# Sixteen-byte offsets for the operands of an MLP's matmuls

## The chip, the cores and the metric

One core of a Trainium2 chip runs the whole program. The metric is the device time of one execution in microseconds, the median of several runs.

## The reference

Retention attention feeds two MLPs. The second one, which the change touches, is in fp32:

```python
def _moe2_ref(x, w_in, w_out):          # x: 2304 x 512, w_in: 512 x 2048, w_out: 2048 x 512
    h = x @ w_in
    neg, pos = h <= -1.0, h >= 1.0
    g = np.where(pos, h, np.where(neg, 0.0, (h + 1.0) ** 2 / 4.0))
    return (g @ w_out).astype(np.float32)
```

## The kernel before

All work is issued in an order written out by hand, the list ORDER: a word such as `hp.7.2` calls the step `hp_` with arguments 7 and 2. Engines take their instructions in that order, and semaphores between tiles do the rest. Attention and the first MLP fill the first 276 us or so; the second MLP runs from there to the end, at first together with the last of the first MLP.

Every fp32 product of the second MLP is made of three TensorE matmuls, since each operand is split in a high and a low part of type fp32r (high times low, low times high, high times high). The matrices are multiplied by a scheme with seven products instead of eight per 2x2 blocks: operands are stored as seven combinations, and the weights' combinations were computed earlier and put into DRAM (`wid` and `wod`, one piece for each of eight groups of 256 hidden units).

There are 32 main steps, four blocks of 512 tokens by eight groups. Step s does:

- `wi` and `wo` (both through `load_for` and `load14`) load 14,336 bytes a partition, the seven combinations of one group's weights, high and low, with one DMA on SP's queue. Three buffers hold weights of each kind. A new load takes the buffer of the step three before, so the weights rotate through homes named by pool and tag: w0 and w1 of pool w1i and wo2 of pool wos for the weights in, wo0 and wo1 of pool wos and ln of pool act1 for the weights out. Near the end weights out come to the homes of weights in, too.
- `hp_` (its matmuls are L753) makes 42 matmuls: the weights are the stationary operand, 128x128, and a tile `xs` of tokens the moving one, 256 columns.
- `ha`, `hA`, `hB`, `hr_`, `hm`, `hq`, `hg`, `hf` on ScalarE and VectorE apply the activation and make the seven combinations of its result.
- `hh` on ScalarE and `hl` on VectorE split them into the gates' high and low part, two tiles that `ghl_tiles` gives out. They alternate with the step: tags w0 and w1 of pool w1o in even steps, w2 and w3 in odd ones.
- `pp` (L841, through `product`) makes 42 matmuls: now the gates are stationary, and the weights out the moving operand, 256 columns.

In the order list the matmuls of `pp` for an earlier step lie between those of `hp_`, a few at a time. The last 256 tokens have steps of their own: `tp` (L923) for the first product and `tj` (L841 again) for the second, with gates made by `ty` and `tz`.

Where a buffer lies modulo 256 bytes follows from the pads of 64 and 224 bytes at the foot of the two memory stacks, from tile sizes, which are multiples of 256 for nearly all tiles, and from the offset `o` in `load14`, counted in elements of four bytes. As built, all stationary tiles of the second MLP start at 0 modulo 256 (weights in, gates) and all moving ones at 192 (tokens, weights out). In each matmul the moving operand less the stationary one is then 192, and slices inside the tiles are multiples of 512 bytes.

Of the kernel before, what the change touches and what calls it, by code (L numbers as in the profile page):

```python
# [12 lines left out]
F32R = mybir.dt.float32r  # L13
# [10 lines left out]
DM = H * D  # L24
F1, F2 = 1024, 2048
P = 128
# [194 lines left out]
def net(ctx: ExitStack, tc: tile.TileContext, qk_t, kv, w_in1, w_out1, g_ln, w_in2, w_out2, masks, decay, out):  # L221
# [11 lines left out]
    w1i = ctx.enter_context(tc.tile_pool(name="w1i", bufs=1, side="right"))  # L233
    w1o = ctx.enter_context(tc.tile_pool(name="w1o", bufs=1, side="right"))
    const = ctx.enter_context(tc.tile_pool(name="const", bufs=1, side="right"))
    act1 = ctx.enter_context(tc.tile_pool(name="act1", bufs=1, side="right"))
# [173 lines left out]
    raw_w, wd, yd, rd, w_in1_sb, wo1, ws, w2x, w1s = {}, {}, {}, {}, [None] * KD, [None] * (C1 // 2), {}, {}, {}  # L410
# [255 lines left out]
    def load14(kind, p, home):  # L666
        pool, tag = home
        n, pools = 2 * 7 * 2 * P, {"w1i": w1i, "wos": wos, "act1": act1}
        x = pools[pool].tile([P, n + 64 * (pool != "act1")], F32R, tag=tag, name=kind)
        o = {"w1i": 0, "wos": 16, "act1": 0}[pool] if kind == "wi" else {"w1i": 48, "wos": 0, "act1": 0}[pool]  # L670
        x = x[:, o : o + n]
        x = x.rearrange("p (w i f) -> p w i f", w=2, f=2 * P)
        nc.sync.dma_start(x.bitcast(F32), (wid if kind == "wi" else wod)[p])
        resident[kind][p] = x, (pool, tag)

    def load_for(kind, s):
        full = len(resident[kind]) == 3
        if kind == "wo" and s == len(slots) - 1:
            home = resident["wi"].pop(slots[s - 2][1])[1]
        else:  # L680
            home = resident[kind].pop(slots[s - 3][1])[1] if full else homes[kind, s]
        load14(kind, slots[s][1], home)
# [9 lines left out]
    @step  # L692
    def wt(p):
        kind, old = {4: ("wi", 1), 5: ("wi", 0), 6: ("wo", TAIL[0]), 7: ("wo", TAIL[1])}[p]
        load14("wo", p, resident[kind].pop(old)[1])
# [112 lines left out]
        nc.vector.tensor_tensor(out=g[:, o], in0=g[:, x], in1=g[:, y], op=op)  # L808

    def ghl_tiles(i, n):  # L810
        return [w1o.tile([P, 7, n, P], F32R, tag=f"w{2 * (i % 2) + w}", name="g" + "hl"[w]) for w in range(2)]

    @step
    def hh(s, k):
        if k == 0:
            ghl[s] = ghl_tiles(s, 2)
        i = slice(4 * k, 4 + 3 * k)
        nc.scalar.activation(ghl[s][0][:, i], gs[s][:, i], AF.Copy)  # L818
# [189 lines left out]
    with tc.manual_schedule():  # L1008
        for word in ORDER.split():
            name, *args = re.split("[.]", word.rstrip("+"))  # L1010
            f = steps[name] if name in steps else steps[name + "_"]
# [43 lines left out]
```

## Time and profile before

| | us |
|---|---|
| median of 3 runs | 661.94 (661.71 to 668.92) |
| profiled execution | 662.21 |
| its span | 660.0 |
| granted TensorE clock, mean | 0.999 |
| TensorE busy | 651.8 |
| VectorE busy | 529.3 |
| ScalarE busy | 446.1 |

The span goes from the first to the last instruction of the profiled execution. TensorE's work is counted in matmuls (PE) and weight loads into the array (PEld), which run beside the matmuls. Matmuls overlap as well: one of 276 ns begins about 113 ns after the one before it, so a time from start to start says more than a duration.

### The profile page before, as it was taken

The numbers are of one execution on the slowest core, as the hardware profiler recorded it, in microseconds if no ns is written. First come the engines' busy times: TensorE is split into PE (matmuls) and PEld (weight loads), VectorE is DVE, ScalarE is ACT, GpSimd is POOL, SyncE is SP. The second block draws the span as 40 slices with busy tenths as digits, with TensorE's granted clock in tenths as the row PEclk, the third lists the DMA queues.
The fourth block names the chain that finished last, engine by engine and source line by source line (L and its number), as shares of the span: only waits on it lengthen the run. The fifth ranks groups of instructions, "written<-read, shape, count | busy, mean of one in ns | idle before, by whom it ended". The sixth has DMA issues, their size and how long they took to land.

```text
span 660.0 us, 14294 instructions
## 1 busy us (share of the span) xinstructions
PE 651.8 (99%) x5697; PEld 615.5 (93%) x5697; DVE 529.3 (80%) x1037; ACT 446.1 (68%) x806; POOL 180.4 (27%) x180
## 2 busy tenths in 40 slices
PE   9999999999999999999999999999999999999997
PEld 7888898998989898899999999999999999999997
DVE  4999898897997789936588879687888877766887
ACT  5678786768776776875667765676756766666642
POOL 5896765545565458510000000000000000000000
PEclk9999999999999999999999999999999999999999
DMA  8986386687986767999895756967497463677986
GB/s 321 392 301 256 131 293 263 230 274 273 409 295 222 249 266 265 387 337 404 324 411 200 308 221 214 345 236 279 184 355 281 182 223 118 250 302 292 366 305 236
DMA packets 34802, 184.85 MB, mean 280 GB/s; under 512 B 3760, under 2 KB 8496, under 8 KB 28208
## 3 DMA queue, kind: packets, MB, share of 16 engines
q1 hardware_dynamic: 34448, 183.65, 75.1%
q8 instruction: 45, 0.74, 0.4%
q10 hardware_dynamic: 288, 0.30, 0.2%
q14 instruction: 21, 0.17, 0.1%
HBM read 143.04 MB, written 40.89 MB: 279 GB/s over the span
## 4 chain that ended last, share of the span: by engine, by line
PE 80%; DVE 11%; DMA 5%; issue 1%; POOL 1%; ACT 1%; SPq 0%; DVEq 0%; POOLq 0%; ACTq 0%
PE bank L841 27%; PE bank L753 24%; PE bank L528 8%; PE bank L630 8%; PE bank L923 3%; PE bank L280 2%; DVE ws L455 2%; DVE ws L497 2%; PE bank L322 2%; PE bank L352 2%; DMA st<-in_w_in 2%; PE bank L340 2%; PE bank L600 1%; DVE sm L538 1%; DMA wod<-ws 1%; DMA kv<-in_kv 1%
## 5 line engine op out<-in xcount | busy, mean ns | idle before, releaser
L753 PE MATMUL bank<-xs,wi 128*128 128x256 f32 x1344 | 177.0, 280 | 0.7 <-ACT hc L770 0.7
L753 PEld LDWEIGHTS bank<-xs,wi 128*128 128x128 f32 x1344 | 164.3, 188 | 2.2 <-ACT hc L770 1.3
L841 PE MATMUL bank<-wo,gh 128*128 128x256 f32 x896 | 160.9, 278 | 0.0
L841 PEld LDWEIGHTS bank<-wo,gh 128*128 128x128 f32 x896 | 136.4, 189 | 0.0
L841 PE MATMUL bank<-wo,gl 128*128 128x256 f32 x448 | 124.8, 279 | 0.0
L528 PE MATMUL bank<-wi,x 128*128 128x512 f32 x432 | 104.7, 397 | 0.0
L630 PE MATMUL bank<-ln,wo 128*128 128x256 f32 x864 | 103.1, 279 | 0.6 <-DVE xf L379 0.6
L630 PEld LDWEIGHTS bank<-ln,wo 128*128 128x128 f32 x864 | 100.8, 188 | 1.8 <-DVE xf L379 0.8
L528 PEld LDWEIGHTS bank<-wi,x 128*128 128x128 f32 x432 | 79.4, 188 | 17.5 <-issue 0.8
L841 PEld LDWEIGHTS bank<-wo,gl 128*128 128x128 f32 x448 | 84.1, 188 | 0.2
L824 DVE TENSOR_TENSOR gl<-gs,gh 128x1024 fp32r<-128x1024 f32 (+1 forms) x64 | 69.3, 1088 | 15.5 <-ACT gh L818 15.3
L440 POOL TENSOR_TENSOR y<-y,st 128x512 int32<-128x512 int32 x48 | 66.6, 1391 | 47.1 <-DVE y L436 30.3
L770 ACT COPY hc<-bank 128x512 f32<-128x512 f32 x64 | 37.6, 588 | 61.7 <-PE bank L753 59.7
L818 ACT ACTIVATE gh<-gs 128x1024 fp32r<-128x1024 f32 x64 | 60.9, 953 | 1.9 <-PE bank L841 1.2
L808 DVE TENSOR_TENSOR gs<-gs 128x256 f32<-128x256 f32 x128 | 51.8, 421 | 1.2
L800 DVE TENSOR_TENSOR gs<-hc,r 128x512 f32<-128x512 f32 x64 | 43.2, 689 | 11.8 <-ACT r L792 10.8
L509 POOL TENSOR_TENSOR ws<-ws 128x256 f32<-128x256 f32 x41 | 36.2, 891 | 23.0 <-DVE ws L455 12.3
L497 DVE TENSOR_TENSOR ws<-ws,hi 128x1024 fp32r<-128x1024 f32 (+1 forms) x32 | 40.9, 1290 | 0.9 <-ACT hi L486 0.8
L784 ACT ACTIVATE r<-hc 128x512 f32<-128x512 f32 x64 | 40.0, 630 | 1.6 <-DVE gs L800 0.8
L792 ACT ACTIVATE r<-r 128x512 f32<-128x512 f32 x64 | 39.5, 627 | 1.7 <-DVE r L788 1.7
L788 DVE TENSOR_SCALAR r<-r 128x512 f32<-128x512 f32 x64 | 26.8, 423 | 15.4 <-ACT r L784 14.8
L774 DVE TENSOR_TENSOR hc<-hc,sn 128x512 f32<-128x512 f32 x32 | 22.0, 688 | 17.8 <-ACT hc L770 17.8
(109 smaller groups left out, 1006.7 us busy)
## 6 DMA issues: line engine op xcount, KB each, us to landing
wo<-wod SPq DMA_DIRECT2D x27, 1792.0 KB, 9.0
wi<-wid SPq DMA_DIRECT2D x23, 1792.0 KB, 8.8
st<-in_w_in SPq DMA_DIRECT2D x24, 512.0 KB, 5.7
st<-in_w_out SPq DMA_DIRECT2D x24, 512.0 KB, 5.4
kv<-in_kv SPq DMA_DIRECT2D x18, 512.0 KB, 7.2
qk<-in_qk_t SPq DMA_DIRECT2D x18, 512.0 KB, 6.2
wod<-hi SPq DMA_DIRECT2D x8, 896.0 KB, 6.7
wod<-ws SPq DMA_DIRECT2D x8, 896.0 KB, 6.0
```

The costliest lines, as they stand in the source:

```text
L440: nc.gpsimd.tensor_tensor(out=yd[u].bitcast(I32), in0=yd[u].bitcast(I32), in1=raw_w[u][:, :, 0].bitcast(I32), op=ALU.add)
L497: (nc.gpsimd if kind < 2 and u % 2 and not alt else nc.vector).tensor_tensor(out=lo, in0=r, in1=hi.bitcast(F32), op=ALU.subtract)
L528: nc.tensor.matmul(hp, a[:, kk, :], w[:, fs], start=(n == 0), stop=(n == 3 * KD - 1))
L630: nc.tensor.matmul(px[:, mm, :], w[:, ms], a[:, f, :], start=(n == 0), stop=(n == 3 * C1 - 1))
L753: nc.tensor.matmul(hp[s][:, half], w[:, u, SLOT[o], kk * P : (kk + 1) * P], x[:, a, kk], start=(n in (0, 3) and half == 0 and k == 0), sto ...
L784: nc.scalar.activation(hr[s, k], hc[s][:, 1 - k], AF.Relu, bias=0.5, scale=0.5)
L792: nc.scalar.activation(hr[s, k], hr[s, k], AF.Square)
L800: nc.vector.tensor_tensor(out=g, in0=h, in1=r, op=ALU.max)
L808: nc.vector.tensor_tensor(out=g[:, o], in0=g[:, x], in1=g[:, y], op=op)
L818: nc.scalar.activation(ghl[s][0][:, i], gs[s][:, i], AF.Copy)
L824: nc.vector.tensor_tensor(out=l[:, i], in0=gs[s][:, i], in1=h[:, i].bitcast(F32), op=ALU.subtract)
L841: nc.tensor.matmul(po[key][:, half], g[a][:, x, t], w[:, u, y], start=(first and j == 0 and half == lead), stop=(last and j == 2), skip_gr ...
```

## The change

In `load14` the offset goes by the tag of the buffer instead of by its pool: weights in stay at offset 0 in w0, move to 4 elements (16 bytes) in w1, and from 16 to 12 elements in wo2; weights out stay at 48 elements in w0 and w1 and at 0 in wo0 and ln, and move to 4 in wo1 and 8 in wo2. In `ghl_tiles` the tiles get the whole size that their buffers have, and the gates of odd steps start 8 elements (32 bytes) in. The tail's own gates (`ty`) stay where they were. Nothing else changes.

```diff
         x = pools[pool].tile([P, n + 64 * (pool != "act1")], F32R, tag=tag, name=kind)
-        o = {"w1i": 0, "wos": 16, "act1": 0}[pool] if kind == "wi" else {"w1i": 48, "wos": 0, "act1": 0}[pool]
+        o = {"w0": 0, "w1": 4, "wo2": 12}[tag] if kind == "wi" else {"w0": 48, "w1": 48, "wo0": 0, "wo1": 4, "wo2": 8, "ln": 0}[tag]
         x = x[:, o : o + n]
...
     def ghl_tiles(i, n):
-        return [w1o.tile([P, 7, n, P], F32R, tag=f"w{2 * (i % 2) + w}", name="g" + "hl"[w]) for w in range(2)]
+        o, size = 8 * (i % 2), 7 * n * P
+        tiles = [w1o.tile([P, 2 * DM * 2], F32R, tag=f"w{2 * (i % 2) + w}", name="g" + "hl"[w]) for w in range(2)]
+        return [x[:, o : o + size].rearrange("p (y n k) -> p y n k", n=n, k=P) for x in tiles]
```

## Rows read from the trace of the kernel before

**Rows 1.** The page: busy time of the engines, and the chain that ended last.
```profile
PE 651.8 (99%) x5697; PEld 615.5 (93%) x5697; DVE 529.3 (80%) x1037; ACT 446.1 (68%) x806; POOL 180.4 (27%) x180
...
PE 80%; DVE 11%; DMA 5%; issue 1%; POOL 1%; ACT 1%; SPq 0%; DVEq 0%; POOLq 0%; ACTq 0%
```

**Rows 2.** The chain in order of time: start us, us, what.
```profile
348.29 1.36 PE bank L753 x12
397.99 1.41 PE bank L753 x12
```

**Rows 3.** Windows, TensorE alone: stretch, us, busy (matmuls), clock, DMA share, GB/s.
```profile
276.00:277.90 1.90, 1.90 (x16) 1.00 1.03 430
277.90:292.70 14.80, 14.80 (x127) 1.00 0.96 356
292.70:397.20 104.50, 103.82 (x900) 1.00 0.79 308
397.20:519.20 122.00, 122.00 (x1037) 1.00 0.73 267
519.20:530.20 11.00, 11.00 (x96) 1.00 0.45 166
530.20:541.80 11.60, 11.60 (x101) 1.00 0.57 215
541.80:584.10 42.30, 42.30 (x371) 1.00 0.60 224
584.10:593.40 9.30, 9.30 (x81) 1.00 0.73 269
593.40:638.50 45.10, 45.10 (x399) 1.00 0.86 323
638.50:656.00 17.50, 17.50 (x148) 1.00 0.74 271
```

**Rows 4.** Timeline of TensorE about two changes of pace: start us, us, matmuls.
```profile
397.02 0.38 PE L841 MATMUL bank<-wo,gl 128*128 128x256 f32 x1
397.24 0.40 PE L841 MATMUL bank<-wo,gh 128*128 128x256 f32 x2
...
519.50 0.97 PE L753 MATMUL bank<-xs,wi 128*128 128x256 f32 x6
520.31 0.28 PE L841 MATMUL bank<-wo,gl 128*128 128x256 f32 x1
...
520.65 0.28 PE L841 MATMUL bank<-wo,gl 128*128 128x256 f32 x1
```

**Rows 5.** Timeline of TensorE, the groups with the first and the last hold-up.
```profile
276.21 2.01 PE L753 MATMUL bank<-xs,wi 128*128 128x256 f32 x14
...
651.31 1.66 PE L841 MATMUL bank<-wo,g 128*128 128x256 f32 x11
```

**Rows 6.** Landing of weights in, then out; timeline of one load and its first use.
```profile
DMA to landing us min/median/max: 7.3/8.8/16.6
...
DMA to landing us min/median/max: 7.0/9.0/14.8
...
568.87 0.41 SPq L673 DMA_DIRECT2D wi<-wid  x1
...
580.11 0.62 PE L753 MATMUL bank<-xs,wi 128*128 128x256 f32 x4
```

**Rows 7.** All waits of TensorE's matmuls from 275 us on: us, times, longest.
```profile
PE bank L600 <- DVE ln L616: 1.3, 1, 1.3
PE bank L753 <- ACT hc L770: 0.7, 1, 0.7
```

**Rows 8.** Groups of ScalarE by shape: casts to address 0, then to 192.
```profile
L818 ACT ACTIVATE gh<-gs 128x1024 fp32r<-128x1024 f32 x32 | 34.0, 1063 | 1.9 <-PE bank L841 1.2 <-PE bank L630 0.5
...
L486 ACT ACTIVATE hi<-ws 128x1024 fp32r<-128x1024 f32 x16 | 16.9, 1055 | 5.3 <-DMA wid<-hi 3.1 <-DMA wod<-hi 2.2
```

**Rows 9.** Timeline of TensorE in the warm-up, bf16 matmuls.
```profile
9.75 4.97 PE L280 MATMUL bank<-zero 128*128 128x256 bf16 x44
```

## The prediction

> **What bounds the kernel now.** The page's first part comes first: TensorE is busy 99% of the span, and the chain that ended last is TensorE's for 80% of it [rows 1]. The windows over the second MLP (from 276 us on) say more: TensorE is busy in 379.3 of 380 us at a granted clock of 1.00 [rows 3], and there it waited for results by 2.0 us in all, never for a DMA [rows 7]. So this part of the kernel lasts as long as its matmuls take one after another. I read next how long one takes, because the change touches nothing but addresses of their operands.
>
> The chain in order of time shows two paces for the same group of twelve matmuls, same line and same shape: 1.36 us at 348.29 and 1.41 us at 397.99 [rows 2]. That is 113.3 and 117.5 ns from one matmul to the next. The windows give the same in long stretches [rows 3]: 397.2 to 519.2 holds 1037 matmuls, 117.6 ns each, and 593.4 to 638.5 holds 399, 113.0 ns each. (Up to three matmuls at the edges of a window are counted twice; without them these are 117.8 and 113.6.) Both stretches mix the two products, L753 and L841, are at clock 1.00 and without idle time. I take 113.3 and 117.7: 4.4 ns between them.
>
> A pace, once taken, stays. Slow are 277.9 to 292.7, 397.2 to 519.2, 530.2 to 541.8, 584.1 to 593.4 and 638.5 to 656; the five others hold the fast one most of the time [rows 3]. Inside a stretch the weights change every 42 matmuls and the gates every 42, without effect. The pace changes where TensorE was held up for a moment: the matmul at 397.02 takes 0.22 us to the next one instead of 0.11 and the slow pace follows; the one at 519.50 comes after a hold-up, six matmuls last until 520.31 (0.81 us: 0.22 for the first, 118 ns each for the others), and then three take 0.34 us, the fast pace [rows 4]. I counted 28 such hold-ups in the second MLP, from the one at 276.21 to the one in the group at 651.31 [rows 5], by intervals over 130 ns between matmul starts: after 21 of them the fast pace follows, after 7 the slow one.
>
> My reading: matmul and next weight load read SBUF together, both with addresses that advance; in one alignment in time they disturb each other and in the other not, and a hold-up draws anew. What the trace can't show is how this depends on the addresses, since now every stationary tile stands at 0 and every moving one at 192 modulo 256.
>
> **The change part by part.** Instructions, their order, semaphores and queues are the same in number: 3,048 matmuls in the second MLP (1,344 of L753, 1,512 of L841, 192 of the remainder L923), 50 weight loads. Tile sizes in memory don't move either: a gates tile of 2,048 elements has the size that the buffer already had for the first MLP's weights.
>
> *Weights in.* Twelve of 32 steps keep distance 192, twelve (tag w1) get 176, eight (wo2) get 208. *Weights out and gates.* Together they give L841 distances 192, 160, 208, 176 and 224. Counted through the order list over the 3,048 matmuls: 1,143 keep 192; 786 have 176; 678 have 208; 420 have 160; 21 have 224. Where before no distance ever changed, it now changes 248 times, mostly where the order goes from L753 to L841 and back.
>
> The bounds of what this can do to the paces come from rows 3. The slow stretches add up to 14.8 + 122.0 + 11.6 + 9.3 + 17.5 = 175.2 us, at 117.7 ns some 1,490 matmuls, about 100 of them the first MLP's. By the intervals between starts 1,430 of the second MLP's are slow and 1,578 fast; the rest follow a hold-up. If all became fast: 1,430 x 4.4 ns = 6.3 us saved. If the other 1,578 became slow: 6.9 us lost. DVE and ACT can feed the fast pace: the fast stretches hold no idle TensorE beyond 0.7 us [rows 3].
>
> Which value between? I take each change of distance as a small hold-up: it moves one stream against the other by 16 to 64 bytes, so the pace is drawn anew, 248 times instead of 28, and a bad draw no longer lasts 1,037 matmuls. With the draw that the trace shows (7 of 28 slow) the slow share falls from 48% to 25%: 752 matmuls slow instead of 1,430, which saves 678 x 4.4 ns = 3.0 us. Against it stands the settling: five matmuls at the slow pace at 519.50 before the fast one [rows 4]. A shift of some bytes should settle sooner than a full stop; between 1 and 5 I take 1.5, nearer the small end: 248 x 0.75 x 1.5 x 4.4 ns = 1.2 us (0.8 to 4.1). Sum: -3.0 + 1.2 = -1.8 us.
>
> *Loads to odd addresses.* Weight loads into w1, wo1 and wo2 now land at 16, 208, 224 and 240 modulo 256 instead of 0 or 192. No row shows a DMA to a start that is no multiple of 64. Nearest are loads to 0 (wi, median 8.8 us) and to 192 (wo, 9.0 us) [rows 6]: 0.2 us for an offset, hidden, as TensorE waits for no DMA [rows 7]. A gain is excluded, since no one waits for them. The far bound is the slowest load in the trace, 16.6 us [rows 6]. The load issued at 568.87 is first used at 580.11 [rows 6]: 11.2 us. At 16.6 this one would stop TensorE for 5.4 us. I take 0, from the 0.2.
>
> Beside these rows: the Trainium skill ("DMA: Bandwidth & Descriptors", How a descriptor splits into AXI transactions) says that transactions of 256 bytes start at multiples of 256, so that an unaligned stretch needs one more. By it a partition's 14,336 bytes would need 57 instead of 56 at 16 as at 192, an estimate of 0.2 us in 9.0; the two medians agree with that.
>
> *Gates 32 bytes on, in odd steps.* ScalarE's cast of 1,024 elements takes 1063 ns to an address 0 (L818) and 1055 ns to 192 (L486) [rows 8]; I take nothing, and a difference of 10 ns on 64 casts would lie beside TensorE's work.
>
> **How that adds up.** The profiled execution took 662.21 us, 2.2 outside its span of 660.0; the median of the runs is 661.94, 0.3 less, so the profile's stretches stand for it. 661.94 - 1.8 = 660.1 us.
>
> **The rivals.**
> *Nothing changes.* The pace may depend on time alone and not on addresses: weights and gates change with each step, at addresses thousands of bytes apart, and the pace persists [rows 3]. Against it: those moves were all multiples of 256. The draws then fall as before: 661.9.
> The Trainium skill ("TensorE: Matmul & The Clock Gate", Part 2, Step-by-step) gives this result from another side: weight loads have a read port of their own and take nothing from a running matmul. Had it no exception, there would be one pace; the trace has two at the same clock, so I don't lean on it more than this rival says.
>
> *All slow.* At distances 176, 208 or 160 the disturbed alignment may be the only stable one, and since L753 and L841 alternate, it would pull those at 192 along. For it: 192 may be a good distance, where others were never seen. It ends slower once more than 48% of the matmuls are slow; at 100%: 661.9 + 6.9 = 668.8.
>
> *All fast.* The reverse: one of the new distances allows only the fast pace and, as no change from fast to slow is seen without a hold-up, it resets the others within some matmuls. 661.9 - 6.3 = 655.6.
>
> *A third pace.* The warm-up's bf16 matmuls of the same width run 44 in 4.97 us [rows 9], some 109 ns each (first to last start: 4.70 us, 43 intervals), 4 ns under the fast pace. If new distances reached that, 3,048 x 4 = 12 us more would go: 643. Nothing shows a matmul of these operands under 113.
>
> *Late weights.* If starts at 16 modulo 256 stretch a load by half, loads with 11.2 us to their use come late. Besides the one at 568.87 I found two with as little, and at 16.6 us each stops TensorE by about 5: 667 to 677.
>
> **How the numbers follow.** Forecast (mixed paces, 658 to 664): 0.38. Nothing changes (661 to 663): 0.25. All slow, or mostly: 0.14. All fast, or nearly: 0.15. Late weights: 0.05. Third pace: 0.03. The likeliest gives 660.1. The range takes in all fast (655.6 less 0.6 for the clip of settling and stops) and all slow short of its upper half: 655.0 to 668.8. Outside stay half of all slow, late weights and the third pace, 0.15, and a rest. Measurement can tell about 2% from no change, 13.2 us. Faster than 648.7 needs the third pace: 0.02. Slower than 675.1 needs late weights or a slower pace than either: 0.03. Within 2%: 0.95.
>
> **What would show it.** Right: in the windows after 276 the matmuls of a 40 us window lie between those of the two paces, and the chain shows groups of 1.36 and 1.41 alternating within a few us instead of stretches of 100 us; TensorE's waits stay at 2 us. Nothing changes: long pure stretches again. All slow or all fast: one number throughout. Late weights: waits for a DMA on wi or wo. The prediction fails if one distance has a pace that isn't in this trace, or if hold-ups fall otherwise and draw another long stretch by luck: one of 120 us is worth 4.6 us.

## The result, and the profile after

The changed kernel takes 669.51 us (median of 18 runs, 667.13 to 674.65) against 661.31 us for the kernel before (median of 18 runs, 657.85 to 668.92, taken beside it). The ratio is 1.0121, with a 95% interval of 1.0099 to 1.0144: the change makes the kernel 1.2% slower. I had forecast 660.1 us. The ratios and intervals here and below are estimated over the runs and differ a little from quotients of two medians. In later sessions the kernel before had medians of 666.39 and 665.20 us on one chip and 663.16 on another, so further down each kernel is compared with the runs of before beside it.

The profiled execution took 668.30 us, its span is 666.2, 6.2 us longer than the span of before. TensorE's busy time grew from 651.8 [rows 1] to 656.4 us. The page's first part:

```profile
PE 656.4 (99%) x5697; PEld 620.3 (93%) x5697; DVE 531.2 (80%) x1037; ACT 445.5 (67%) x806; POOL 180.5 (27%) x180
```

Instructions that write or read the weights in, then the weights out (durations min/median/max in ns, first and last start in us; time to landing):

```profile
L753 PE MATMUL bank<-xs,wi x1344: 276/280/388, 277.0 to 620.8; 128*128 128x256 f32 x192
...
DMA to landing us min/median/max: 7.2/8.6/16.1
```

```profile
L843 PE MATMUL bank<-wo,g x168: 276/276/357, 642.1 to 662.1; 128*128 128x256 f32 x168
...
DMA to landing us min/median/max: 7.0/9.0/15.0
```

The line of `product` has moved from L841 to L843. The second MLP goes from 277.0 to 662.1 us, 385.1 us; before it went from the matmul at 276.21 [rows 5] to the last one at 655.9, 379.7 us. So 5.4 of the 6.2 us arise there.

Did something new have to be waited for? All waits of TensorE's matmuls from 275 us on, in us, times, longest:

```profile
PE bank L600 <- DVE ln L616: 1.3, 1, 1.3
PE bank L753 <- ACT hc L770: 0.7, 1, 0.7
PE bank L843 <- DMA wo<-wod: 0.4, 1, 0.4
```

Hardly. The first two waits are those of before [rows 7], one of 0.4 us on a weight load is new (the run with the gates moved alone, where no load has a new address, has one of 0.3), and loads land as they did [rows 6]. The time is in the pace. Windows of TensorE alone (stretch, us, busy, matmuls in brackets, granted clock, DMA share, GB/s):

```profile
350.00:390.00 40.00, 40.00 (x342) 1.00 0.63 237
400.00:440.00 40.00, 40.00 (x344) 1.00 0.78 279
440.00:480.00 40.00, 40.00 (x343) 1.00 0.61 235
480.00:518.00 38.00, 38.00 (x328) 1.00 0.86 311
595.00:635.00 40.00, 40.00 (x343) 1.00 0.83 297
```

Two of the same windows before:

```profile
350.00:390.00 40.00, 40.00 (x355) 1.00 0.65 240
400.00:440.00 40.00, 40.00 (x342) 1.00 0.74 267
```

Before, such stretches alternated: 292.7 to 397.2 and 593.4 to 638.5 at the fast pace, 397.2 to 519.2 at the slow one [rows 3]. Now all hold 342 to 344 (or 328 in 38 us), at the same granted clock. The chain in order of time shows that it isn't one slow pace, though:

```profile
425.97 1.42 PE bank L753 x12
427.39 1.37 PE bank L843 x12
428.76 1.42 PE bank L753 x12
...
431.21 1.36 PE bank L753 x12
...
437.11 1.43 PE bank L843 x12
438.54 1.38 PE bank L753 x12
```

Twelve matmuls take 1.36 to 1.38 us or 1.42 to 1.43, turn by turn, as [rows 2] showed in long stretches. By the addresses of the operands (those that the built kernel gives its tiles, put beside the matmuls of the trace in their order), those at 427.39, 431.21 and 438.54 have distance 192 (moving less stationary start, modulo 256), and those at 425.97, 428.76 and 437.11 have 176. The pace goes with the distance.

I sorted all intervals between the starts of successive matmuls of the second MLP in the trace by distance (intervals of 135 ns and more, the hold-ups, left out, and those where the distance changes kept apart):

| distance | before: count, mean ns | after: count, mean ns |
|---|---|---|
| 192 | 3,004, 115.5 | 1,095, 114.8 |
| 176 | | 760, 118.9 |
| 208 | | 605, 118.7 |
| 160 | | 342, 119.0 |
| 224 | | 20, 118.4 |
| at a change of distance | | 188, 118.5 |

Fast intervals (113 or 114 ns) are 768 of the 1,095 at 192, and 27 of the 1,727 at the four other distances.

The averages over all are 115.46 and 117.34 ns: 1.88 ns x 3,010 intervals = 5.7 us, which is the 5.4 us by which the second MLP grew, within 0.3.

### The profile page after: what moved, and what is told of

Same layout as the page of the kernel before. It is cut to its first block, busy times and chain, and to the rows that moved or that the text cites. A ratio compares the mean times of both kernels' runs of the same rounds, so it can differ in the third digit from the quotient of the medians.

```text
span 666.2 us, 14294 instructions
## 1 busy us (share of the span) xinstructions
PE 656.4 (99%) x5697; PEld 620.3 (93%) x5697; DVE 531.2 (80%) x1037; ACT 445.5 (67%) x806; POOL 180.5 (27%) x180
## 4 chain that ended last, share of the span: by engine, by line
PE 80%; DVE 12%; DMA 3%; issue 2%; ACT 1%; POOL 1%; SPq 0%; DVEq 0%; ACTq 0%; POOLq 0%
PE bank L843 25%; PE bank L753 24%; PE bank L528 9%; PE bank L630 8%; PE bank L925 3%; PE bank L280 2%; DVE ws L455 2%; DVE ws L497 2%; PE bank L322 2%; PE bank L352 2%; DMA wo<-wod 2%; PE bank L600 2%; PE bank L340 2%; DVE sm L538 1%; DVE y L436 1%
## 5 line engine op out<-in xcount | busy, mean ns | idle before, releaser
L753 PE MATMUL bank<-xs,wi 128*128 128x256 f32 x1344 | 179.2, 281 | 0.7 <-ACT hc L770 0.7
L753 PEld LDWEIGHTS bank<-xs,wi 128*128 128x128 f32 x1344 | 166.4, 188 | 2.2 <-ACT hc L770 1.2
L843 PE MATMUL bank<-wo,gh 128*128 128x256 f32 x896 | 163.5, 280 | 0.0
L843 PEld LDWEIGHTS bank<-wo,gh 128*128 128x128 f32 x896 | 137.1, 189 | 0.0
L843 PE MATMUL bank<-wo,gl 128*128 128x256 f32 x448 | 125.7, 280 | 0.0
L843 PEld LDWEIGHTS bank<-wo,gl 128*128 128x128 f32 x448 | 84.6, 189 | 0.1
```

The costliest lines, as they stand in the source:

```text
L753: nc.tensor.matmul(hp[s][:, half], w[:, u, SLOT[o], kk * P : (kk + 1) * P], x[:, a, kk], start=(n in (0, 3) and half == 0 and k == 0), sto ...
L843: nc.tensor.matmul(po[key][:, half], g[a][:, x, t], w[:, u, y], start=(first and j == 0 and half == lead), stop=(last and j == 2), skip_gr ...
```

## The experiments

Three theories were on record. A: each distance has a pace of its own, and 192 is the only one of those seen that has a fast one. B: a change of distance in the stream of matmuls costs time. C: starts off 0 and 192 cost, in weight loads or in writes.

**All starts 32 bytes on, distances kept.**

```diff
-    pad(ctx.enter_context(tc.tile_pool(name="left", bufs=1, side="left")), 64)
-    pad(ctx.enter_context(tc.tile_pool(name="right", bufs=1, side="right")), 224)
+    pad(ctx.enter_context(tc.tile_pool(name="left", bufs=1, side="left")), 96)
+    pad(ctx.enter_context(tc.tile_pool(name="right", bufs=1, side="right")), 192)
```

> Both stacks stand 32 bytes higher, so every tile of the kernel starts 32 bytes on modulo 256, gates and weights in at 32, tokens and weights out at 224, and every distance (moving less stationary) stays 192. Theory A (each distance has its own pace of the matmuls; in the changed kernel's trace 192 has 113.3 or 117.7 ns, and 176, 208 and 160 have 118.4 to 119.1): the same as before, 661.3 within 1.5, matmuls of the second MLP 115.5 on average with long stretches of either pace. Rival B (a change of distance in the stream costs time by itself): no change of distance here, the same, 661.3. Rival C (the start addresses themselves matter, for weight loads that land off 0 or 192, or for writes of the gates off 0): slower, 665 to 670.

Measured: 666.18 us against 666.39 for before beside it, ratio 1.0001 (0.9975 to 1.0028). Windows:

```profile
350.00:390.00 40.00, 40.00 (x355) 1.00 0.63 242
400.00:440.00 40.00, 40.00 (x342) 1.00 0.78 283
440.00:480.00 40.00, 40.00 (x342) 1.00 0.59 231
595.00:635.00 40.00, 40.00 (x355) 1.00 0.86 314
```

The same two paces in the same long stretches as before. Starts of 32 and 224 instead of 0 and 192 do nothing by themselves; the distance is what all have kept.

**The gates' part alone** (the offset in `load14` as before).

> The gates' part of the change alone: odd steps' gates 32 bytes on, 672 of 3,048 matmuls at distance 160 instead of 192, 132 changes of distance in the stream. Theory A: those 672 at 119.0 instead of 115.5 ns cost 2.4 us; the 2,376 at 192 keep 115.5 or come to 114.7 as in the changed kernel's trace, which gives back up to 1.9: 661.8 to 663.7. Rival B: 132 of the changed kernel's 197 changes of distance, so 132/197 of its 8.2 us: 666.8. Rival C (weight loads to odd addresses): none here, 661.3.

Measured: 665.10 us against 666.39, ratio 0.9995 (0.9970 to 1.0021): no difference, where B wanted 5.5 us more. The chain:

```profile
433.50 1.37 PE bank L753 x12
434.87 1.44 PE bank L843 x12
...
445.97 1.36 PE bank L753 x12
...
449.71 1.41 PE bank L843 x12
```

The twelve at 434.87 have distance 160 and take 1.44 us; their neighbours at 192 take 1.36 to 1.37, and so does everything at 192 in this stretch, which before was slow from 397.2 to 519.2 [rows 3]. By intervals: 606 at 160 with 119.9 ns, 2,272 at 192 with 114.2 instead of 115.5. After a return to 192 the first four intervals are 117.0, 116.0, 114.4 and 113.7 ns on average. So here an excursion does end a slow stretch, as I had forecast, and pays for that with the matmuls that it puts at 160: in this profile 606 x 4.4 = 2.7 us lost, 2,272 x 1.2 = 2.8 us won.

**Two scans of the distance in steps of 16 bytes.** Weights in and gates get a common offset that changes every four steps; the moving operands stay.

```diff
-        o = {"w1i": 0, "wos": 16, "act1": 0}[pool] if kind == "wi" else {"w1i": 48, "wos": 0, "act1": 0}[pool]
+        o = (want - {"w1i": 0, "wos": 192, "act1": 192}[pool]) % 256 // 4
...
-        load14(kind, slots[s][1], home)
+        load14(kind, slots[s][1], home, OFF[s // 4] if kind == "wi" else 192)
...
+        o, size = OFF[min(i // 4 + 1, 7)] // 4, 7 * n * P
```

> One look at many distances in one run: weights in and gates start at the same offset for about four steps on end, 0, 16, 32, 48, 64, 80, 96, 112, the moving operands stay at 192, so the distance goes through 192, 176, 160, 144, 128, 112, 96, 80, from one plateau of some 40 us to the next. Theory A: each plateau has a pace of its own; 176 and 160 at 118 to 119 ns with no stretch of 113.3, the unseen ones anywhere from 113 to 123, all in all slower than before by 2 to 8 us. Rival B: within a plateau the paces 113.3 and 117.7 as before, at every distance, mean 115.5; slow intervals only near the 89 changes.

> The same with offsets 128, 144, 160, 176, 208, 192, 224, 240: distances 64, 48, 32, 16, 240, 0, 224, 208. Theory A: each has its own pace, 208 at 118 to 119 ns; if some distance holds 113.3 throughout, it would make a better kernel than both. Rival B: two paces as before at each of them, mean 115.5.

Measured, one run each: 671.13 and 674.84 us. Windows within plateaus, first scan (distances 176, 144, 112 and 80), then second (48, 16, 0 and 208):

```profile
339.00:362.00 23.00, 23.00 (x194) 1.00 0.61 240
404.00:442.00 38.00, 38.00 (x319) 1.00 0.75 269
482.00:522.00 40.00, 40.00 (x336) 1.00 0.80 292
586.00:640.00 54.00, 54.00 (x459) 1.00 0.84 304
```

```profile
343.00:365.00 22.00, 22.00 (x191) 1.00 0.62 244
406.00:444.00 38.00, 38.00 (x327) 1.00 0.75 272
484.00:524.00 40.00, 40.00 (x336) 1.00 0.80 290
588.00:640.00 52.00, 52.00 (x426) 1.00 0.81 296
```

With two or three matmuls counted twice at a window's edges, 459 in 54 us are 118 ns each and 426 in 52 us are 123 ns. By intervals: 80 has 118.2, 96 119.6, 112 119.5, 128 118.5, 144 119.9, 160 119.0, 176 119.2; 208 122.4, 224 118.3, 240 118.4, 0 119.9, 16 117.8, 32 116.7, 48 117.0, 64 116.4. None of the fifteen other distances has 113.3 ns on average. One of them, 64, has both paces as 192 has: 47 of its 149 intervals are 113 or 114 ns, in unbroken rows between hold-ups. B's two paces at every distance are not there; of the three theories A fits. Distance 208 shows that a pace can be slower than any in the trace of before: 247 of its 596 intervals are 130 ns. The same starts, 240 and 192, have 118.4 ns in the changed kernel, where the stream stays there for 6 to 24 matmuls at a time, so a distance doesn't fix a number.

**The weights in alone, the weights out alone.**

```diff
+        o = {"w0": 0, "w1": 4, "wo2": 12}[tag] if kind == "wi" else {"w1i": 48, "wos": 0, "act1": 0}[pool]
```

```diff
+        o = {"w1i": 0, "wos": 16, "act1": 0}[pool] if kind == "wi" else {"w0": 48, "w1": 48, "wo0": 0, "wo1": 4, "wo2": 8, "ln": 0}[tag]
```

> The weights in alone: 576 of 3,048 matmuls at distance 176, 384 at 208, no gates and no weights out moved, 164 changes of distance. Theory A (a distance has its own pace: 192 alone is fast, or slow after an unlucky hold-up; and a return to 192 settles on the fast one within four matmuls, as the gates' run showed with 117.0, 116.0, 114.4, 113.8 ns): 960 at 118.8, the 2,088 at 192 at about 114.4, so 115.8 on average, against 115.5 in the profile of before: within 2 us of it, no clear difference. Rival B (each change of distance costs): 164 of them at 42 ns, 6.9 us slower. Rival C (weight loads to 16 and 240 modulo 256 land late): waits of the matmuls on weights, 5 us and more slower.

> The weights out alone: 525 matmuls at 208, 63 at 224, 106 changes. Theory A: 588 at 118.7, 2,460 at 114.4: 115.2 on average, 1 us faster than the profile of before, within 2 us of it in the runs. Rival B: 106 x 42 ns = 4.5 us slower. Rival C: 2 us and more slower.

Measured: 664.25 us and 664.30 against 665.20, ratios 0.9993 (0.9968 to 1.0018) and 0.9975 (0.9950 to 1.0001). Neither is slower, so B and C fall in the size that they had forecast (6.9 and 5 us for the weights in, 4.5 and 2 for the weights out): weight loads to 16, 208, 224 and 240 cost nothing that shows, nor do 164 changes of distance. By intervals the weights in give 860 at 176 and 208 with 118.5 ns on average and 1,992 at 192 with 114.1; the weights out 534 at 208 and 224 with 119.0, and 2,373 at 192 with 115.0. Each part alone breaks even. All three together do not. My reading of the counts: 62% of the matmuls then stand at slow distances, and there are few left at 192 that can win.

**Rarer excursions.**

```diff
+        o, size = 8 * (i % 4 == 1), 7 * n * P
```

> Gates 32 bytes on in one step of four only (336 matmuls at 160, 68 changes), all else at 192. Theory A: 336 at 119.9, the 2,712 others at 114.0, since long slow stretches are cut by the next excursion: 114.7 on average instead of 115.5 in the profile of before, 2.5 us faster than before, and more (up to 5) where before drew long slow stretches. Rival B: 68 changes cost 2.9 us. If excursions as rare as this don't cut slow stretches: 115.9, 1 us slower.

Measured: 663.84 us against 665.20, ratio 0.9982 (0.9954 to 1.0009): no difference. The theory expected 114.7 ns and got 115.9: 2,636 intervals at 192 with 115.4. Slow stretches came again between excursions, each of the long ones after a hold-up, as in the chain, which stands at 192 throughout:

```profile
346.44 1.47 PE bank L753 x12
347.90 1.41 PE bank L843 x12
349.31 1.41 PE bank L753 x12
...
359.21 1.41 PE bank L753 x12
```

**A scan around 192 in steps of four bytes** (as the scans above, with offsets 252, 4, 8, 12, 0, 252, 248, 244).

> One look at distances around 192 in steps of four bytes, about four steps of the second MLP each: 196, 188, 184, 180, 192, then 196, 200, 204. Theory A, if the pace goes with the distance in whole 16-byte lines: all those from 192 to 204 behave like 192, 180 to 188 like 176 (118.8). If it goes byte by byte: paces between 113.3 and 119 that grow with the way from 192. Rival D (only the start at a multiple of 32 or 64 bytes counts): none of the seven has the fast pace.

Measured: 668.43 us, one run. Windows at 188, 180, 192, 196 and 204:

```profile
343.00:366.00 23.00, 23.00 (x196) 1.00 0.60 238
407.00:444.00 37.00, 37.00 (x328) 1.00 0.79 284
471.00:480.70 9.70, 9.70 (x88) 1.00 0.52 192
482.00:522.00 40.00, 40.00 (x337) 1.00 0.81 291
586.00:640.00 54.00, 54.00 (x477) 1.00 0.87 317
```

None of the expected patterns. By intervals 180 has 113.5 ns and 204 has 113.9, both fast, and what lies between them is slow but for 192: 184 118.3, 188 118.4, 196 119.5, 200 119.5. Distance 180 had 11 of 449 intervals over 115 ns, 192 in the same run 143 of 362.

**The changed kernel again, distance 180 or 204 throughout, and the change in steps of 12 bytes.** All on one chip. For 180:

```diff
+        o = {"w1i": 3, "wos": 19, "act1": 0}[pool] if kind == "wi" else {"w1i": 48, "wos": 0, "act1": 0}[pool]
...
+        o, size = 3, 7 * n * P
```

The tail's gates move by the same; for 204 the offsets are 61, 13 and 61. The change in steps of 12 bytes:

```diff
+        o = {"w0": 0, "w1": 3, "wo2": 13}[tag] if kind == "wi" else {"w0": 48, "w1": 48, "wo0": 0, "wo1": 3, "wo2": 0, "ln": 0}[tag]
...
+        o, size = 3 * (i % 2), 7 * n * P
```

> The changed kernel once more, beside three variants on one chip. Theory A: 1,884 of 3,048 matmuls at 176, 208, 160 and 224 with 118.2 to 119.0 ns, 1,164 at 192 with 114.8: 117.3 ns on average, 358 us of matmuls, where the runs of before have 115.5 (fast draws) to 117.7 (slow draws): 668 to 671, slower than before by 3 to 8 us according to what before draws there.

> All weights in and all gates, the tail's too, 12 bytes on: distance 180 in all 3,048 matmuls of the second MLP, no change of distance. Theory A, each distance has its own pace and 180 only the fast one (113.5 ns on its plateau in the scan): 113.5 ns throughout, 2.0 us per 1,000 matmuls less than the profile of before, so 6 us faster than that: 655 to 657, with less spread. Rival B (the plateau in the scan was fast by a lucky draw, as 192 is at times): long slow stretches as before, 660 to 666. Rival C (starts off 16 bytes cost the loads or the writers): waits on weights or gates, slower than before.

> The same with starts 12 bytes short of the next 256 (244 modulo 256): distance 204 throughout. Theory A: 113.9 ns as in the scan, 655 to 658. Rival B: as before, 660 to 666.

> The change in steps of 12 bytes instead of 16: weights in at 0, 12 and 244, weights out in wo1 12 bytes on, gates of odd steps 12 bytes on; distances 192 (1,395 matmuls), 180 (996) and 204 (657), 173 changes of distance, nearly as many as in the changed kernel. Theory A: all three distances can hold the fast pace, and a change away and back ends a slow stretch: 113.8 to 114.5 ns, 656 to 659. Rival B (changes of distance cost by themselves): slower than before by 7 us.

Measured, against 663.16 us for before beside them:

| kernel | us | ratio to before | mean interval, ns |
|---|---|---|---|
| changed kernel | 670.31 | 1.0118 (1.0078 to 1.0158) | 117.5 |
| 180 throughout | 658.27 | 0.9947 (0.9917 to 0.9977) | 113.5 |
| 204 throughout | 659.56 | 0.9967 (0.9941 to 0.9993) | 113.6 |
| steps of 12 bytes | 663.94 | 1.0013 (0.9982 to 1.0044) | 115.4 |

Windows of 180 throughout, then of 204:

```profile
350.00:390.00 40.00, 40.00 (x355) 1.00 0.62 234
400.00:440.00 40.00, 40.00 (x356) 1.00 0.76 276
440.00:480.00 40.00, 40.00 (x356) 1.00 0.69 268
595.00:635.00 40.00, 40.00 (x353) 1.00 0.84 314
```

```profile
400.00:440.00 40.00, 40.00 (x356) 1.00 0.77 270
595.00:635.00 40.00, 40.00 (x354) 1.00 0.85 309
```

The fast pace throughout, also in the stretch from 400 to 480 that was slow before, and across all hold-ups. Distance 180 is faster than both kernels, by 0.5% against before on this chip. Steps of 12 bytes missed the 656 to 659 that A expected. Its chain has a slow stretch:

```profile
428.88 1.36 PE bank L753 x12
430.25 1.39 PE bank L843 x12
...
433.39 1.42 PE bank L753 x12
434.81 1.41 PE bank L843 x12
...
446.10 1.41 PE bank L753 x12
...
448.58 1.37 PE bank L753 x12
```

By the addresses, all from 428.7 to 448.4 us stands at distance 192. The pace falls in the middle of the twelve at 430.25, with no hold-up: there gates and weights out both move 12 bytes on, to 12 and 204, and keep their distance. The L753 between them, at 0 and 192, are slow with them, and stay so until weights in at 12, distance 180, come at 448.4. The whole run by the starts of both operands:

| stationary, moving | distance | intervals, mean ns | of 113 or 114 ns |
|---|---|---|---|
| 0, 192 | 192 | 1,071, 115.6 | 521 |
| 12, 192 | 180 | 929, 113.8 | 845 |
| 244, 192 | 204 | 345, 115.6 | 211 |
| 12, 204 | 192 | 223, 118.1 | 1 |
| 0, 204 | 204 | 249, 117.3 | 0 |

With the moving operand at 204 the fast pace is not there, at distances 192 and 204, which have it with the moving operand at 192 (204 throughout: 2,848 of 3,005 intervals are fast). So the pace isn't the distance's alone: where the moving operand starts counts too, and a group at a bad start can pull those after it along. The moving starts seen fast are 192 and 224. In the three scans and in 180 and 204 throughout it stayed at 192, so what they say holds for that start.

## Why the prediction was wrong, point by point

**What bounds the kernel, and the two paces: right.** TensorE's stream is what counts, pace after pace; loads, waits and writers stayed hidden, as costed at nothing.

**The step that failed** is "I take each change of distance as a small hold-up ... so the pace is drawn anew", together with the share that it used for it, 7 of 28, at every distance. The draw is one of distance 192. At 176, 208, 160 and 224 no fast pace was there to be drawn. Of the 3,048 matmuls 1,884 left 192, with 197 changes of distance (I had miscounted them as 1,905 and 248). In the profile their intervals average 118.8 ns against 115.5 before. 1,884 x 3.3 ns = 6.2 us lost. The prediction's last paragraph names this case, a distance with "a pace that isn't in this trace", as one in which it fails; neither the sum nor the range had a term for it.

**The effect that I forecast exists and is small.** The 1,164 matmuls of the changed kernel that stayed at 192 went from 115.5 to 114.8 ns, 0.8 us won, where I had 3.0 us on all matmuls. 6.2 - 0.8 = 5.4 us is what the second MLP lost. That an excursion ends a slow stretch is clearest in the gates' run; with excursions in every fourth step only, hold-ups began new slow stretches in between. The settling (1.5 matmuls at the slow pace, 6.6 ns) was about right in the gates' run: 3.7, 2.7, 1.1 and 0.4 ns over 113.3 are 8 ns a return. In the changed kernel it was nearly twice what I had: 118.7, 116.8, 114.7 and 114.7 ns, 12 ns a return.

**The rival "all slow"** (0.14, 668.8 us) came nearest, and by its mechanism, new distances without the fast pace. Half of it is wrong: it let the others pull 192 along, which the changed kernel's table contradicts (the run in steps of 12 bytes shows that this does happen, at a moving start of 204), and its price assumed that 117.7 ns is the slowest pace there is. The range ended there, too. I had given the bounds from above only by rows at distance 192; a distance never seen had no upper bound from them, and should have had a wider one.

**The median and the profile** differ more than I allowed for: the pair of profiles is 6.1 us apart, the medians 8.2. The profiled run of before lies 0.9 over its median and that of after 1.2 under its own. Runs of before spread over 11 us, and 180 throughout over 8. Part of that goes with the granted clock: 180 throughout has 655.2 to 658.3 us in the seven runs with a mean of 0.999 or 1.000, and 659.5 to 663.4 in the five with 0.995 to 0.997. The runs of before beside them still spread from 657.9 to 667.3 us at 0.999 or 1.000; that the rest is draws of long slow stretches fits, but these runs left no traces to show it.

**The weight loads** cost nothing: 8.6 and 9.0 us against 8.8 and 9.0 [rows 6]. By the rule that the prediction took from the Trainium skill ("DMA: Bandwidth & Descriptors", How a descriptor splits into AXI transactions) a load to 16 or 240 would need one transaction more than one to 0. That is an estimate of 0.2 us more for 14 of 23 loads of weights in; their median fell by 0.2, so no run here shows it. The page speaks of what a transaction reads, and the moved starts are where the loads write.

**The rule about the read ports** (the Trainium skill, "TensorE: Matmul & The Clock Gate", Part 2, Step-by-step: a weight load takes nothing from the running matmul) would have given 661.9. It leaves no room for what was measured: the same matmul with its load beside it, at clock 1.00, takes 113.5 ns at distance 180 and 119.9 at 0, and as the moving operand starts at 192 in both, only the load's address differs. How the load does it, no run shows.

**What stays open**: why these distances, and why not with the moving operand at 204. The fast ones found are 180, 192 and 204, twelve bytes apart, and 64 at times. That the two read streams meet in memory is my reading; the runs show the dependence on the starts, not where it arises.

## What to carry to other kernels

Where a stream of matmuls is the bound and its pace changes at a constant clock without waits, compare the start addresses of the moving and the stationary operand modulo 256, and scan their distance within one run, a plateau of steps for each value, in steps of four bytes. A distance found so holds for the moving start of the scan: move the operand that the scan moved. Keep one good distance for all, rather than many: mixing moved 62% of the matmuls here to slower ones. And a range needs more than the two ends of what a trace shows when the change goes where the trace has never been.

## What the runs showed of the hardware that I had not expected

- Matmuls of 256 fp32r columns, each with a new 128x128 weight load, run at 113.5 to 122.4 ns on average depending on the distance of their operands' starts modulo 256, with the moving one at 192 (shift of all starts by 32: no effect). With the moving one at 204 they had 118.1 ns at distance 192 and 117.3 at 204.
- At 192 there are two paces that last, 113.3 and 117.7 ns; at 180 only the fast one lasted in 3,002 intervals (96% of them 113 or 114 ns), across 39 hold-ups.
- Loads of weights in to starts at 0, 16 and 240 modulo 256 had a median of 8.6 us, 8.8 us when all started at 0.
